# Down and output products with the weights standing and 512 tokens streamed, in a gated mix of linear attention and a GEGLU network

## The chip, the cores and the metric

The kernel runs on one core of one Trainium2 chip. Its engines are TensorE (PE in the profile, with its weight loads shown as PEld), VectorE (DVE), ScalarE (ACT), GpSimd (POOL) and SyncE (SP), which here only issues DMAs. The metric is device microseconds for one launch. Most executions of one kernel agree within 0.3%.

## The reference, cut to what matters

```python
x = A_x                                              # 2048 tokens x 640
g = sigmoid((x * gate_w).sum(-1, keepdims=True))     # one number per token
a = linear_attention(x, wqkv, w_phi) @ wo            # 32 heads of 20
b = (gelu(x @ w_gate) * (x @ w_up)) @ w_down         # hidden size 1728
return g * a + (1 - g) * b                           # 2048 x 640, bf16
```

The change touches the last two products, the one with `wo` and the one with `w_down`, which the kernel adds up in the same accumulator, the factor (1 - g), and the way the result goes to memory. The attention part is divided by its denominator and multiplied by g / (1 - g) before, so that one multiplication by (1 - g) closes both.

## The kernel before, in words

The 2048 tokens are 16 tiles of 128, and four tiles are one block. All is written out by hand: a small scheduler (`_Sched`) emits each instruction in program order on its engine's queue and puts a semaphore wait ahead of it for what it reads and overwrites. The order of the program is therefore the order of every queue, and a waiting instruction holds all that stand behind it on its engine. DMAs of the SP queue go round 16 lanes.

The program has three stages. `attention_state` projects keys, values and queries and builds the state of the linear attention. `ffn` first runs gate and up for 4 blocks x 14 chunks of the hidden size (counter `n`, 0 to 55): for each chunk ten 128x512 matmuls (L469), a GELU on ACT (L857) and a product on DVE (L861), which leaves the hidden activations transposed in `hT`, with the hidden index on the partitions and the block's 512 tokens along the row. Chunk 13 holds only 64 hidden rows; its product (L851) is written to partitions 0 to 63 and again to 64 to 127, half of the tokens each (`odd`) in blocks 0 to 2. Between the chunks stand the attention's last steps: `q_turn(t)` (a transposing DMA on SP), `num(t)` (eleven matmuls at L878 into PSUM banks 2 and 3, three DVE operations that leave `Og`, and a transposing DMA that leaves `goT`). After the fourth chunk of block 0 `kv_state` reads the attention state out of banks 3 and 4, and `gates` computes the gate column `Gm`.

The third stage is `down_pair`, called for two token tiles at a time, eight times. All its matmuls (L921) have 64 rows. The two halves of the array work side by side: rows 0 to 63 for one accumulator bank, rows 64 to 127 for the other, and such a couple is called a slot below. The standing operand is a 64x128 piece of `hT` (or `goT`); the streamed one is 320 columns of `wd_sb` (or `wo_sb`). A group is one pair of banks. Each group is opened (14 chunks of `hT` and 5 of `goT`: 19 slots) and later closed with the halves swapped (13 and 5: 18 slots). ACT scales the bank by `Gm[:, t]`, one number per partition (L936), into `outsb`, and one DMA per two tiles writes 320 KB out. The last pair has three groups of 320, 224 and 96 columns, and DVE takes half of their evacuations (L933).

Of the kernel before, what the change touches and what calls it, by code (L numbers as in the profile page):

```python
# [3 lines left out]
P = 128  # L4
BF16 = mybir.dt.bfloat16
F32 = mybir.dt.float32
AF = mybir.ActivationFunctionType
ALU = mybir.AluOpType
# [99 lines left out]
class _Kernel:  # L108
    S, D, H, DH, F = 2048, 640, 32, 20, 1728
    KD = D // P  # L110
    NT = S // P
    TB = 4
    BT = TB * P
    NB = S // BT
    NFC = 14
# [35 lines left out]
    def alloc(self):  # L151
        nc = self.nc
        S, D, KD, NT, BT, NFC, DH = self.S, self.D, self.KD, self.NT, self.BT, self.NFC, self.DH
        T = nc.alloc_sbuf_tensor
        self.xT = T("xT", [P, KD, S], BF16)
        self.wo_sb = T("wo_sb", [P, KD, D], BF16)
        self.wg_sb = T("wg_sb", [P, KD, 13 * P], BF16)
        self.wu_sb = T("wu_sb", [P, KD, 13 * P], BF16)
        self.wgu_sb = T("wgu_sb", [P, KD, P], BF16)
        self.wd_sb = T("wd_sb", [P, NFC, D], BF16)  # L160
        self.Eq = T("Eq", [P, NT, self.G * P], BF16)
        self.KV = T("KV", [P, self.G, 72], BF16)
        self.hmask = T("hmask", [P, 3, self.HG], BF16)
        self.mask = T("mask", [P, KD, 8], BF16)
        self.ident = T("ident", [P, P], BF16)
        self.gz = T("gz", [P, P], BF16)
        self.gcol = T("gcol", [P, NT], F32)
        self.gtmp = T("gtmp", [P, NT], F32)
        self.Gm = T("Gm", [P, NT], F32)
        self.Gr = T("Gr", [P, NT], F32)  # L170
        self.BD = T("BD", [P, KD, 4 * DH], BF16)
        self.wphi_sb = T("wphi_sb", [P, KD, DH], BF16)

        def place(lists):
            size = {"b": 0}
            plans = []
            for items in lists:
                c = 0
                for name, shape, dt in items:
                    n = mybir.dt.size(dt)  # L180
                    for s_ in shape[1:]:
                        n *= s_
                    c = (c + 31) // 32 * 32
                    plans.append((name, shape, dt, c))
                    c += n
                size["b"] = max(size["b"], c)
            arena = T("arena%d" % len(self._arenas), [P, size["b"]], mybir.dt.uint8)
            self._arenas.append(arena)
            base = nc.lookup_mloc(arena).addr
            for name, shape, dt, c in plans:  # L190
                setattr(self, name, nc.alloc_sbuf_tensor_at(name, shape, dt, offset=base + c))
        self._arenas = []
        place([
            [("w3", [P, KD, self.K0 + 2 * self.H * self.E], BF16)],
            [("hT0", [P, NFC, BT], BF16), ("gl", [P, 3, BT], BF16)],
        ])
        place([
            [("Ek", [P, self.NSE, self.G * P], BF16), ("vaug", [P, self.NSV, self.G, 64], BF16)],
            [("hT1", [P, NFC, BT], BF16), ("RH", [P, 2, 2, self.H], F32), ("Dq", [P, self.NSQ, 2, self.G * self.HG], F32),
             ("Sb", [P, 2 * self.G * self.HG, 5], F32), ("Sc", [P, 2 * self.G * self.HG, 2], F32),  # L200
             ("between", [P, 1472], F32), ("Sa", [P, 2 * self.G * self.HG, 10], F32)],
        ])
        place([
            [("Eq0", [P, self.G * P], BF16), ("Dk", [P, self.NSE, 2, 2 * self.G * self.HG], F32)],
            [("hT2", [P, NFC, BT], BF16)],
        ])
        place([
            [("wkT", [P, KD, D], BF16), ("wqT", [P, KD, D], BF16), ("room", [P, 504], F32),
             ("wref", [P, KD, self.H], F32), ("rest", [P, 600], F32), ("xtok", [P, self.TB, D], BF16)],
            [("ahead", [P, 2 * KD, D], BF16), ("kstage", [P, self.HM * DH], F32)],  # L210
            [("upl", [P, len(self.LATE), BT], F32), ("qstage", [P, self.HM * DH], F32)],
            [("under", [P, 4464], F32), ("upf", [P, len(self.UP), BT], F32)],
            [("goT", [P, self.NGO, KD, P], BF16), ("Og", [P, 2, D], BF16), ("outsb", [P, 4, D], BF16)],
        ])
        self.ps = nc.alloc_psum_tensor("ps", [P, 4096], F32)

    def bank(self, b, n=512):
        return self.ps[:, b * 512:b * 512 + n]
# [603 lines left out]
    def gateup(self, b, c, banks):  # L822
        sc = self.sc
        xs = lambda kt: self.xT[:, kt, b * self.BT:(b + 1) * self.BT]
        xr = [("xT", t) for t in range(4 * b, 4 * b + 4)]
        old = (self.oldw, self.oldk, self.oldq, [("xT", t) for t in range(12)])[b]
        hT, hk = self.hT(b, c), b
        slot = self.gn % 3
        self.gn += 1
        if c < 13:  # L830
            i = 0 if c < 7 else 1
            early = c in self.UP + self.LATE
            done = early and b == 0
            if done and c != self.LATE[0]:
                banks = banks[::-1]
            for w, wk, bk in ((self.wg_sb, "wg", banks[0]), (self.wu_sb, "wu", banks[1]))[:1 if done else 2]:
                for kt in range(self.KD):
                    key = self.upheld(c)[1] if early and wk == "wu" else (wk, i, kt)
                    self.mm(bk, 0, 512, w[:, kt, c * P:(c + 1) * P], xs(kt), kt == 0, kt == self.KD - 1, xr + [key])
            up, upk = (self.upheld(c)[0], ("upf", c)) if done else (self.bank(banks[1]), ("ps", banks[1]))  # L840
            self.gateup_evac(b, c, banks[0], slot, up, upk, old)
        else:
            bk = banks[1 if b else 0]
            for kt in range(self.KD):
                self.mm(bk, 0, 512, self.wgu_sb[:, kt, :], xs(kt), kt == 0, kt == self.KD - 1, xr + ["wgu0", "wgu1"])
            sc.op("act", lambda e: e.activation(self.gl[64:128, slot, :], self.ps[0:64, bk * 512:bk * 512 + 512],
                                                AF.Gelu_apprx_tanh),
                  reads=[("ps", bk)], writes=[("gl", slot)], guard=self.oldw)
            for r in (0, 1):
                odd = lambda v: v if b == 3 else v.rearrange("p (u r q) -> p u r q", r=2, q=P)[:, :, r, :]  # L850
                sc.op("dve", lambda e: e.tensor_tensor(  # L851
                    odd(hT[64 * r:64 * r + 64, :]), odd(self.ps[64:128, bk * 512:bk * 512 + 512]),
                    odd(self.gl[64:128, slot, :]), ALU.mult),
                    reads=[("ps", bk), ("gl", slot)], writes=[("hT", hk, c, r)], guard=old)

    def gelu(self, bank, slot):
# [14 lines left out]
    def num(self, t, b):  # L871
# [4 lines left out]
        for g in range(self.G):  # L876
# [18 lines left out]
        sc.dma("sp", lambda e: e.dma_start_transpose(dst, self.Og[:, sl, :]), reads=[("Og", sl)],  # L895
               writes=[("goT", t)], guard=old + list(dead))

    def down_pair(self, t0, banks, last):

        sc = self.sc  # L900
# [25 lines left out]
        def evac(h):  # L926
            for j in (0, 1):
                t, w0, w = parts[h][j]
                bk, dst, g = banks[h][j], self.outsb[:, t % 4, w0:w0 + w], self.Gm[:, t:t + 1]
                rd, wr = [("ps", bk), "Gm"], [("outsb", t % 4, h, j)]  # L930
                was = [("outsb", t % 4, k, (t - t0)) for k in (0, 1)] if last and h < 2 else ()
                if last and j == 1:
                    sc.op("dve", lambda e: e.tensor_scalar(dst, self.bank(bk, w), g, None, op0=ALU.mult), reads=rd, writes=wr,  # L933
                          guard=was)
                else:
                    sc.op("act", lambda e: e.activation(dst, self.bank(bk, w), AF.Copy, scale=g), reads=rd, writes=wr,  # L936
                          guard=was)
# [4 lines left out]
                sc.dma("sp", lambda e: e.dma_start(self.out[t * P:(t + 1) * P, c0:c1], self.outsb[:, t % 4, c0:c1]),  # L942
                       reads=[("outsb", t % 4, h, j) for j in (0, 1)], writes=[("out", t0, h)])
            elif h == nw - 1:
                if t0 < self.TB:
                    rows = self.out[0:self.BT, :].rearrange("(p j) n -> p j n", j=self.TB)[:, t0:t0 + 2, :]
                else:
                    rows = self.out[t0 * P:(t0 + 2) * P, :].rearrange("(j p) n -> p j n", p=P)
                sc.dma("sp", lambda e: e.dma_start(rows[:, :, :], self.outsb[:, os_:os_ + 2, :]),
                       reads=[("outsb", os_ + j, k, j) for j in (0, 1) for k in range(nw)], writes=[("out", t0, h)])  # L950

# [22 lines left out]
    def ffn(self):  # L974
# [6 lines left out]
        n = 0  # L981
        for b in range(self.NB):
            for idx, c in enumerate(order):
# [17 lines left out]
                    if t < 2:  # L1001
                        self.q_turn(t)
                n += 1
        p = [(2, 3), (4, 5)]
        for t in range(0, self.NT, 2):
            final = t + 2 == self.NT
            for _ in self.down_pair(t, p + [(0, 1)] if final else p, final):
                pass
# [44 lines left out]
```

## Time and profile before

| | |
|---|---|
| median of 3 runs | 281.81 us (281.76 to 282.28) |
| the profiled execution | 281.94 us, span 280.7 us |
| granted TensorE clock | 1.00 over the whole span |
| PE busy | 276.9 us, 99% |
| DVE, ACT, POOL busy | 146.8, 106.3, 109.7 us |
| DMA | 24.08 MB, 59848 packets |
| stage of `down_pair` | 198.0 to 279 us |

The page gives busy time by engine, the span in 40 slices, the chain that ended last, and groups of instructions by line. In a timeline a row is a run of like instructions: its start, the time from there to the end of the last, its name and the count. Matmuls are pipelined, so the step from one row's start to the next row's start, divided by the count, is what one matmul really takes of PE; the mean ns in the groups is its latency.

### The profile page before, as it was taken

The numbers are of one execution on the slowest core, as the hardware profiler recorded it, in microseconds if no ns is written. First come the engines' busy times: TensorE is split into PE (matmuls) and PEld (weight loads), VectorE is DVE, ScalarE is ACT, GpSimd is POOL, SyncE is SP. The second block draws the span as 40 slices with busy tenths as digits, with TensorE's granted clock in tenths as the row PEclk, the third lists the DMA queues.
The fourth block names the chain that finished last, engine by engine and source line by source line (L and its number), as shares of the span: only waits on it lengthen the run. The fifth ranks groups of instructions, "written<-read, shape, count | busy, mean of one in ns | idle before, by whom it ended". The sixth has DMA issues, their size and how long they took to land.

```text
span 280.7 us, 6549 instructions
## 1 busy us (share of the span) xinstructions
PE 276.9 (99%) x2729; PEld 168.0 (60%) x2746; DVE 146.8 (52%) x242; ACT 106.3 (38%) x205; POOL 109.7 (39%) x173
## 2 busy tenths in 40 slices
PE   8999999999999999999999999999999999999997
PEld 5566766666665445444444444445677777777785
DVE  1756999999999976655575556655200000000001
ACT  3347978878784322222232223222021121122011
POOL 7937911101068999986666666300000000000000
DMA  7999989300000436554343344731100110110111
GB/s 210 230 221 194 250 274 343 94 2 0 2 0 0 55 75 126 88 112 79 75 79 75 77 79 85 88 75 26 23 22 29 49 47 2 49 49 4 49 49 47
DMA packets 59848, 24.08 MB, mean 86 GB/s; under 512 B 50858, under 2 KB 59306, under 8 KB 59818
## 3 DMA queue, kind: packets, MB, share of 16 engines
q1 hardware_dynamic: 59152, 23.63, 37.3%
q8 instruction: 21, 0.34, 0.5%
q10 hardware_dynamic: 666, 0.03, 0.2%
q14 instruction: 9, 0.07, 0.1%
HBM read 9.04 MB, written 2.62 MB: 42 GB/s over the span
## 4 chain that ended last, share of the span: by engine, by line
PE 99%; issue 0%; ACT 0%
PE ps L469 58%; PE ps L921 29%; PE ps L659 4%; PE ps L482 2%; PE ps L878 2%; PE ps L695 2%; PE ps L735 1%; PE ps L409 1%; PE ps L345 0%; ACT outsb L936 0%; PE ps L742 0%; PE ps L374 0%
## 5 line engine op out<-in xcount | busy, mean ns | idle before, releaser
L469 PE MATMUL ps<-xT,wu_sb 128*128 128x512 bf16 x250 | 62.8, 379 | 0.4
L469 PE MATMUL ps<-xT,wg_sb 128*128 128x512 bf16 x253 | 62.6, 379 | 0.5
L857 ACT ACTIVATE gl<-ps 128x512 bf16<-128x512 f32 x52 | 31.0, 597 | 74.1 <-PE ps L469 70.5
L469 PE MATMUL ps<-w,xT 128*128 128x368 bf16 (+6 forms) x340 | 51.6, 303 | 0.0
L921 PE MATMUL ps<-wd_sb,hT 64*128 64x320 bf16 x648 | 47.0, 296 | 0.0
L469 PEld LDWEIGHTS ps<-xT,wu_sb 128*128 128x128 bf16 x260 | 25.4, 98 | 30.3
L933 DVE TENSOR_SCALAR outsb<-ps,Gm 128x320 bf16<-128x320 f32 (+2 forms) x3 | 1.3, 440 | 78.9 <-ACT outsb L936 78.1
L469 PEld LDWEIGHTS ps<-w,xT 128*128 128x128 bf16 x340 | 32.1, 98 | 14.6
L936 ACT ACTIVATE outsb<-ps,Gm 128x320 bf16<-128x320 f32 (+2 forms) x31 | 14.5, 515 | 66.9 <-PE ps L921 66.9
L469 PEld LDWEIGHTS ps<-xT,wg_sb 128*128 128x128 bf16 x260 | 24.0, 97 | 26.4 <-issue 0.2
L921 PEld LDWEIGHTS ps<-wd_sb,hT 64*128 64x128 bf16 x648 | 31.5, 94 | 12.8 <-DVE Og L890 0.4
L861 DVE TENSOR_TENSOR hT<-ps,gl 128x512 bf16<-128x512 f32 x34 | 23.4, 689 | 23.5 <-PE ps L469 23.5
L627 POOL TENSOR_TENSOR Eq<-Eq,Dq 128x660 bf16<-128x660 bf16 x16 | 21.6, 1350 | 20.0 <-DVE Dq L620 19.3
L686 DVE TENSOR_TENSOR Ek<-Ek,Dk 128x1320 bf16<-128x1320 bf16 x16 | 25.9, 1620 | 0.5
L677 DVE TENSOR_REDUCE Dk<-Ek 128x66 f32<-128x1320 bf16 x16 | 24.3, 1519 | 2.3 <-ACT gcol L541 2.3
L551 ACT ACTIVATE Ek<-ps 128x627 bf16<-128x627 f32 x32 | 20.5, 693 | 6.0 <-PE ps L659 4.5
L608 POOL TENSOR_TENSOR Sa<-Eq 128x660 f32<-128x660 bf16 x16 | 21.9, 1368 | 1.6 <-ACT Ek L551 1.6
L551 ACT ACTIVATE Eq<-ps 128x627 bf16<-128x627 f32 x32 | 20.6, 705 | 2.4 <-PE ps L469 2.4
L301 POOL MEMSET Eq<- 128x1408 bf16 x16 | 19.7, 1297 | 0.0
L921 PE MATMUL ps<-wo_sb,goT 64*128 64x320 bf16 x240 | 19.2, 296 | 0.0
L701 POOL MEMSET Ek<- 128x66 bf16 x11 | 4.3, 393 | 38.2 <-PE ps L695 35.7
L608 POOL TENSOR_TENSOR Sb<-Sa 128x330 f32<-128x330 f32 x16 | 16.7, 1045 | 1.3
(92 smaller groups left out, 255.7 us busy)
## 6 DMA issues: line engine op xcount, KB each, us to landing
out_dram<-outsb SPq DMA_DIRECT2D x7, 320.0 KB, 2.3
wd_sb<-in_B_w_down_dram SPq DMA_DIRECT2D x1, 2080.0 KB, 11.0
wg_sb<-in_B_w_gate_dram SPq DMA_DIRECT2D x5, 224.0 KB, 4.0
wg_sb<-in_B_w_gate_dram SPq DMA_DIRECT2D x5, 192.0 KB, 4.1
wu_sb<-in_B_w_up_dram SPq DMA_DIRECT2D x5, 192.0 KB, 4.3
w<-in_A_wqkv_dram SPq DMA_DIRECT2D x5, 160.0 KB, 4.3
wo_sb<-in_A_wo_dram SPq DMA_DIRECT2D x1, 800.0 KB, 11.5
xtok<-in_A_x_dram SPq DMA_DIRECT2D x2, 320.0 KB, 3.2
```

Source lines behind the costliest of these rows:

```text
L301: self.sc.op("pool", lambda e: e.memset(self.Eq[:, t, :], 1.0), writes=[("Er", t, 0), ("Er", t, 1)])
L469: self.sc.op("pe", lambda e: e.matmul(self.ps[:, bank * 512 + c0:bank * 512 + c0 + n], lhs, rhs, start=first, stop=fin), reads=reads, writ ...
L551: self.sc.op("act", lambda e: e.activation(dst, src, AF.Exp, scale=scale), reads=[("ps", b), ("ps", b + 1)], writes=[(name, sl, s)])
L608: sc.op("pool", lambda e: e.tensor_tensor(out, x, y, ALU.add), reads=reads, writes=writes, guard=old)
L627: self.sc.op("pool", lambda e: e.tensor_tensor(v, v, ratio.unsqueeze(3).to_broadcast([P, G, HG, self.DH]), ALU.mult), reads=[("Dq", sl, 1) ...
L659: self.sc.op("pe", lambda e: e.matmul(out, self.xT[:, kt, t * P:(t + 1) * P], self.w3[:, kt, c:c + 2 * n].rearrange("p (r w) -> p r w", w= ...
L677: self.sc.op("dve", lambda e: e.tensor_reduce(self.Dk[:, se, 0, :].rearrange("p (u h) -> p u h", h=self.HG), self.k_view(se), AX.X, ALU.ad ...
L686: sc.op("dve", lambda e: e.tensor_tensor(v, v, R.rearrange("p (u h) -> p u h", h=self.HG).unsqueeze(3).to_broadcast([P, 2 * self.G, self.H ...
L857: self.sc.op("act", lambda e: e.activation(self.gl[:, slot, :], self.bank(bank), AF.Gelu_apprx_tanh), reads=[("ps", bank)], writes=[("gl", ...
L861: self.sc.op("dve", lambda e: e.tensor_tensor(self.hT(b, c), up, self.gl[:, slot, :], ALU.mult), reads=[upk, ("gl", slot)], writes=[("hT", ...
L921: sc.op("pe", lambda e: e.matmul(self.bank(bk, w), lhs, rhs, start=opens and x == 0, stop=end and not opens, skip_group_check=True), reads ...
L936: sc.op("act", lambda e: e.activation(dst, self.bank(bk, w), AF.Copy, scale=g), reads=rd, writes=wr, guard=was)
```

## The change

For blocks 0 to 2 the two operands change places. A new `down_turned(b, banks)` makes a 64x128 piece of `wd_sb` or `wo_sb` the standing operand, and streams the block's tokens of `hT` or `goT`: 512 at a time for output columns 0 to 511 (two groups, each with two banks of 128 output columns), and twice 256 for the last 128 columns (a third group). Opening and closing have the same 19 and 18 slots, but there are three groups for four tiles instead of four.

The result is now transposed, output column on the partition and token along the row. So the factor (1 - g) has to lie along the row: `gate_rows`, called after chunk 46, writes 12 columns of `Gm` to a scratch tensor in memory and reads it back to all 128 partitions (`GmB`, 6 KB each). DVE multiplies bank by `GmB` into `outT`, five transposing DMAs per block turn `outT` into `outsb`, and one DMA of 640 KB writes the block. `outT` and `GmB` lie in the part of `Eq` that is dead by then.

Block 3 keeps `down_pair`. Its evacuations now wait until block 2's out DMA has read `outsb`. Bank pairs are (4,5), (2,3) in this order, where they were (2,3), (4,5). In chunk 13 of blocks 0 to 2 both halves are now written for all 512 tokens.

```diff
+    def gate_rows(self):
+        n = self.NT - self.TB
+        sc, T = self.sc, self.TB
+        sc.dma("sp", lambda e: e.dma_start(self.gdram.rearrange("(p t) -> p t", p=P), self.Gm[:, 0:n]), reads=["Gm"],
+               writes=["gdram"])
...
+        sc.dma("sp", lambda e: e.dma_start(self.GmB, self.gdram.partition_broadcast(P)), reads=["gdram"],
+               writes=["GmB"], guard=[("Eq", t) for t in (8, 9, 10)])
...
+    def down_turned(self, b, banks):
...
+        parts = [((0, 0, BT), (1, 0, BT)), ((2, 0, BT), (3, 0, BT)), ((4, 0, H), (4, H, H))]
...
+            if c <= NFC:
+                lhs, rhs = self.wd_sb[a:a + 64, c, o * P:(o + 1) * P], self.hT(b, c)[a:a + 64, c0:c0 + w]
...
+                lhs, rhs = self.wo_sb[a:a + 64, k, o * P:(o + 1) * P], self.goT[a:a + 64, t0:t0 + nt, k, :]
...
+        opening, closing = list(range(NFC + 1)) + wos, list(range(NFC)) + wos
+        for opens, steps in ((True, opening), (False, closing)):
+            for h in range(3):
+                for x, c in enumerate(steps):
+                    for r in (0, 1):
+                        mm(r, r if opens else 1 - r, h, c, opens, x, len(steps))
...
+                    g = self.GmB.rearrange("p (q t) -> p t q", q=P)[:, t0:t0 + nt, :]
+                    sc.op("dve", lambda e: e.tensor_tensor(
+                        tiles(self.outT[:, o, c0:c0 + w]), tiles(self.bank(banks[h][j], w)), g, ALU.mult), reads=[("ps", banks[h][j]), "GmB"], writes=[("outT", o, j if h == 2 else 0)],
+                        guard=[("Eq", t) for t in (5, 6)])
+                for o in ((0, 1), (2, 3), (4,))[h]:
+                    sc.dma("sp", lambda e: e.dma_start_transpose(self.outsb[:, :, o * P:(o + 1) * P], self.outT[:, o, :]),
...
+        sc.dma("sp", lambda e: e.dma_start(rows, self.outsb[:, :, :]),
...
-                was = [("outsb", t % 4, k, (t - t0)) for k in (0, 1)] if last and h < 2 else ()
+                was = [("outsb", t % 4, o) for o in range(self.KD)]
...
+                if n == 47:
+                    self.gate_rows()
-        p = [(2, 3), (4, 5)]
-        for t in range(0, self.NT, 2):
+        p = [(4, 5), (2, 3)]
+        for b in range(self.NB - 1):
+            self.down_turned(b, [(4, 5), (2, 3), (0, 1)] if b % 2 == 0 else [(4, 5), (2, 3), (6, 7)])
+        for t in range(self.NT - self.TB, self.NT, 2):
```

More of the change, by code (lines that the diff above doesn't have):

```diff
@@ L215, in alloc @@
         self.ps = nc.alloc_psum_tensor("ps", [P, 4096], F32)
+        self.gdram = nc.dram_tensor("gate_rows", [(NT - self.TB) * P], F32, kind="Internal").ap()
     def bank(self, b, n=512):
@@ L849, in gateup @@
             for r in (0, 1):
-                odd = lambda v: v if b == 3 else v.rearrange("p (u r q) -> p u r q", r=2, q=P)[:, :, r, :]
                 sc.op("dve", lambda e: e.tensor_tensor(
-                    odd(hT[64 * r:64 * r + 64, :]), odd(self.ps[64:128, bk * 512:bk * 512 + 512]),
-                    odd(self.gl[64:128, slot, :]), ALU.mult),
+                    hT[64 * r:64 * r + 64, :], self.ps[64:128, bk * 512:bk * 512 + 512],
+                    self.gl[64:128, slot, :], ALU.mult),
                     reads=[("ps", bk), ("gl", slot)], writes=[("hT", hk, c, r)], guard=old)
@@ L896, in num @@
                writes=[("goT", t)], guard=old + list(dead))
+    def gate_rows(self):
[3 more added lines that the diff above has]
+               writes=["gdram"])
+        self.GmB = self.Eq[:, 7:10, :].rearrange("p a b -> p (a b)")[:, 0:2 * n * P].bitcast(F32)
+        sc.dma("sp", lambda e: e.dma_start(self.GmB, self.gdram.partition_broadcast(P)), reads=["gdram"],
+               writes=["GmB"], guard=[("Eq", t) for t in (8, 9, 10)])
+        self.outT = self.Eq[:, 4:6, :].rearrange("p a b -> p (a b)")[:, 0:self.D * T].rearrange("p (o c) -> p o c", o=self.KD)
@@ new lines, in down_turned, with mm @@
+    def down_turned(self, b, banks):
+        sc, NFC, KD, BT = self.sc, self.NFC - 1, self.KD, self.BT
+        H = BT // 2
+        parts = [((0, 0, BT), (1, 0, BT)), ((2, 0, BT), (3, 0, BT)), ((4, 0, H), (4, H, H))]
+        wos = [NFC + 1 + k for k in range(KD)]
+        def mm(r, j, h, c, opens, x, n):
+            o, c0, w = parts[h][j]
+            bk, a, end = banks[h][j], 64 * r, x == n - 1
+            if c <= NFC:
+                lhs, rhs = self.wd_sb[a:a + 64, c, o * P:(o + 1) * P], self.hT(b, c)[a:a + 64, c0:c0 + w]
+                rd = [("hT", b, c), "wd"] if c < NFC else [("hT", b, 13, r), ("wd13", r)]
+            else:
+                k, t0, nt = c - NFC - 1, self.TB * b + c0 // P, w // P
+                lhs, rhs = self.wo_sb[a:a + 64, k, o * P:(o + 1) * P], self.goT[a:a + 64, t0:t0 + nt, k, :]
+                rd = [("goT", t) for t in range(t0, t0 + nt)] + ["wo"]
+            out = self.bank(bk, w)
+            sc.op("pe", lambda e: e.matmul(out if c <= NFC else out.rearrange("p (t q) -> p t q", q=P), lhs, rhs,
+                                           start=opens and x == 0, stop=end and not opens, skip_group_check=True),
+                  reads=rd, writes=[("ps", bk)] + ([("turn", bk)] if end else []), signal=end,
+                  after=[("turn", bk)] if x == 0 and not opens else ())
+        opening, closing = list(range(NFC + 1)) + wos, list(range(NFC)) + wos
[4 more added lines that the diff above has]
+                        mm(r, r if opens else 1 - r, h, c, opens, x, len(steps))
+                if opens:
+                    continue
+                for j in (0, 1):
+                    o, c0, w = parts[h][j]
+                    t0, nt = self.TB * b + c0 // P, w // P
+                    tiles = lambda v: v.rearrange("p (t q) -> p t q", q=P)
+                    g = self.GmB.rearrange("p (q t) -> p t q", q=P)[:, t0:t0 + nt, :]
[4 more added lines that the diff above has]
+                    sc.dma("sp", lambda e: e.dma_start_transpose(self.outsb[:, :, o * P:(o + 1) * P], self.outT[:, o, :]),
+                           reads=[("outT", o, j) for j in ((0, 1) if h == 2 else (0,))], writes=[("outsb", t, o) for t in range(4)],
+                           guard=self.before_num())
+        if b == 0:
+            rows = self.out[0:BT, :].rearrange("(p j) n -> p j n", j=self.TB)
+        else:
+            rows = self.out[b * BT:(b + 1) * BT, :].rearrange("(j p) n -> p j n", p=P)
+        sc.dma("sp", lambda e: e.dma_start(rows, self.outsb[:, :, :]),
+               reads=[("outsb", t, o) for t in range(4) for o in range(KD)], writes=[("out", b)])
@@ L944, in evac @@
             elif h == nw - 1:
[L945 to L948, printed above, removed]
+                rows = self.out[t0 * P:(t0 + 2) * P, :].rearrange("(j p) n -> p j n", p=P)
                 sc.dma("sp", lambda e: e.dma_start(rows[:, :, :], self.outsb[:, os_:os_ + 2, :]),
```

## The prediction

> **What bounds the kernel now.** I read the page's busy shares and chain first, then PE's timeline at three places, then DVE and SP around the places that the change touches. The page:
>
> ```profile
> span 280.7 us, 6549 instructions
> ...
> PE 276.9 (99%) x2729; PEld 168.0 (60%) x2746; DVE 146.8 (52%) x242; ACT 106.3 (38%) x205; POOL 109.7 (39%) x173
> ...
> PE ps L469 58%; PE ps L921 29%; PE ps L659 4%; PE ps L482 2%; PE ps L878 2%; PE ps L695 2%; PE ps L735 1%; PE ps L409 1%; PE ps L345 0%; ACT outsb L936 0%; PE ps L742 0%; PE ps L374 0%
> ```
>
> PE is the bound from end to end; the products to be changed are 29% of the chain. So only two things can move the time: what one slot takes of PE, and new waits of PE. PE's timeline, in the gate and up stage, in the products, and in the last pair:
>
> ```profile
> 99.24 1.24 PE L469 MATMUL ps<-xT,wg_sb 128*128 128x512 bf16 x5
> ...
> 104.63 0.38 PE L469 MATMUL ps<-xT,wu_sb 128*128 128x512 bf16 x1
> ```
>
> ```profile
> 196.80 1.24 PE L469 MATMUL ps<-xT,wu_sb 128*128 128x512 bf16 x5
> 197.97 3.98 PE L921 MATMUL ps<-wd_sb,hT 64*128 64x320 bf16 x56
> ```
>
> ```profile
> 276.00 1.41 PE L921 MATMUL ps<-wd_sb,xT 64*128 64x224 bf16 x26
> 277.24 0.64 PE L921 MATMUL ps<-wo_sb,Eq 64*128 64x224 bf16 x10
> 277.72 0.72 PE L921 MATMUL ps<-wd_sb,xT 64*128 64x96 bf16 x26
> 278.27 0.38 PE L921 MATMUL ps<-wo_sb,Eq 64*128 64x96 bf16 x10
> ```
>
> The reader is to divide steps between starts by slots. A 512-wide matmul on all rows: (104.63 - 99.24) / 25 = 0.2156 us. A slot of two 224-wide halves: (277.72 - 276.00) / 18 = 0.0956. Of two 96-wide ones: 0.55 / 13 = 0.0423. For 320 columns the out DMAs count best, two pairs of 74 slots apart:
>
> ```profile
> 209.29 0.35 SPq L949 DMA_DIRECT2D out_dram<-outsb  x1
> ...
> 229.40 40.58 SPq L949 DMA_DIRECT2D out_dram<-outsb  x5
> ```
>
> (229.40 - 209.29) / 148 = 0.1359. From 96 to 224 columns the slope is 53.3 / 128 = 0.416 ns a column, which leaves 0.0423 - 96 x 0.000416 = 0.0024 us fixed in each slot. Weight loads cost nothing: two per slot fit even into 0.0423.
>
> DVE in block 0, weight loads at the start of the products, and the DMAs that serve as prices:
>
> ```profile
> 88.46 0.88 DVE L851 TENSOR_TENSOR hT<-ps,gl 64x256 bf16<-64x256 f32 x2
> ...
> 91.63 0.15 DVE L716 TENSOR_TENSOR KV<-ps,hmask 128x2 bf16<-128x2 f32 x1
> ```
>
> ```profile
> 197.97 0.25 PEld L921 LDWEIGHTS ps<-wd_sb,hT 64*128 64x128 bf16 x6 [0.42 <-DVE Og L890]
> ```
>
> ```profile
> out_dram<-outsb SPq DMA_DIRECT2D x7, 320.0 KB, 2.3
> ...
> Eq<-Og SPq DMA_TRANSPOSE x4, 2.6
> ```
>
> **The change part by part. Slots.** Columns streamed are the same: before 4 groups x 37 slots x 320 per block, after 37 x (512 + 512 + 256). Only the number of slots falls, 148 to 111. Before: 148 x 0.1359 = 20.11 us per block. After: a 512-wide slot is not in the trace; I take 0.2156, the row of the same width, and for 256 columns 0.0956 + 32 x 0.000416 = 0.1089, so 37 x (2 x 0.2156 + 0.1089) = 19.98. The gain is 0.13 per block, 0.38 for three; counted as 37 slots saved x 0.0024 x 3 it is 0.27. I take 0.33. Bounds: none of the fixed part left, 512 x 0.416 = 0.2130 and 0.1065, gives 19.70 per block, a gain of 1.2; widths in proportion, 0.1359 x 1.6 = 0.2174 and 0.1087, gives 20.11, a gain of zero. The streamed `goT` has four runs of 128; the nearest row with runs, 2 x 240 columns (L659), has no gap of its own.
>
> **Start of the products.** The first slot begins at 197.97, where 196.80 + 5 x 0.2156 = 197.88 was possible: it waits for `Og` of tile 15 in banks 2 and 3, which the weight-load row names. Opened with (4,5), whose readers end with the product at 193.44 + 0.69, nothing is late; (2,3) come 19 x 0.216 = 4.1 us later. Gain 0.09, no more than this step.
>
> **Chunk 13, on DVE.** Two 64x256 operations (426 ns) become 64x512, as block 3 already has them (694 ns): 0.54 us more per block. Blocks 1 and 2 have DVE gaps of 1.47 us per chunk. In block 0 DVE runs without a gap from 84 to 99 us, and `kv_state` is behind: its last read of bank 4 ends at 91.63 + 0.15 = 91.78, and PE writes that bank at 92.45 (chunk 7: five matmuls before 93.52). The slack of 0.67 shrinks to 0.13. What a released wait takes to reach PE: `Og` ended at 197.69 and the load came at 197.97, 0.28. So the loss is 0 to 0.15; I take 0.10, nearer to the only row. Later banks have over a microsecond. POOL's `q_scale(0)` waits for the DVE step behind chunk 13 and slips 0.54; `q_turn(0)`, issued at 91.83 and landing 3.5 later, has until 98.9.
>
> **Gate rows, on SP.** Two DMAs between `goT(12)` (issued at 179.54) and `q_turn(15)` (182.49): the second waits for the first to land, by the 48 KB row 1.5 us, so `q_turn(15)` slips by about a microsecond and lands, 3.5 us after issue, near 187; beside the 786 KB broadcast perhaps at 190. `num(15)` needs it at 195.4. Nothing, with 5 us of cover; beyond that PE waits one for one. `goT(13)` behind it waits for its `Og` until 186.3 anyway.
>
> **Evacuation.** ACT loses 8 x 523 ns per block; DVE gets four 128x512 products (nearest row L861, 689 ns) and two of 256 (426): 3.6 us in 20, on an engine that is idle after 198.8. A bank is wanted again 5.8 us or more after its closing. Nothing.
>
> **Transposes and the way out.** Five transposes and one DMA a block: 5 x 1.2 us of SP issue in 20 us. What counts is the turn to block 3 at time S, because its evacuations wait for block 2's out DMA. The third group's closing starts 18 x 0.109 = 2.0 before S. With X the time of a 512-wide DVE product, the second group's evacuation begins at S - 1.7 (latency 0.3) and ends at S - 1.7 + 2X; the third's ends one X later, at the earliest S + 0.2 + X. For X = 0.69 that is S + 0.9; SP is held by two transposes until S + 1.4, the fifth lands 2.6 later at S + 4.0, the 640 KB land by S + 7.4 (2.3 for 320 KB, and 1.1 more for the second half). Block 3's first evacuation is due at S + 56 x 0.1359 + 0.3 = S + 7.9, and the last pair opens on its banks at S + 74 x 0.1359 = S + 10.1, less 1.05 for two ACT copies and a signal: S + 8.8. Cover 1.4 us; nothing.
>
> The Trainium skill, "SBUF — State Buffer", section "Door 1: The DMA port swizzle", says that SBUF has lines of 16 bytes and that each access to a new line costs extra; `GmB` is read in steps of 48 bytes. It gives no size; at double time, X = 1.38, the estimate from it stays within the cover, and the sum is the same. The nearest row is L886, which reads PSUM in steps of 84 bytes, 128x32 in 177 ns, against 195 for L620's contiguous 33: no penalty there.
>
> **Sum.** 281.94 - 0.33 - 0.09 + 0.10 = 281.62 for an execution like the profiled one, which was 0.13 above the median: 281.49, 0.11% less. About 0.2% (0.56 us) is what a measurement of this kernel can tell from no change, so this is on the small side of it.
>
> **Rivals.** *The fixed part goes away.* If two wide halves hide it, the slot gain is 1.2 and the time 281.81 - 1.2 - 0.09 + 0.10 = 280.6. For it: it is unknown what the 2.4 ns are. Against: full-row 512-wide matmuls still show them, 0.2156 against 0.2130.
>
> *The last pair waits for block 2's way out (slower).* The third evacuation may end up to S + 2.9 (5.95 for the fifth transpose and the out DMA before S + 8.8); 3X - 1.7 passes that from X = 1.5 us on, and each 0.1 of X beyond costs 0.3. At X = 2.2 PE idles 2.0 us at the opening of the last pair: 283.5. The same happens if transposes and out DMA together take 1.4 us longer than their rows. For it: a strided f32 operand is in no DVE row here, and `outsb` is a strided target. Against: L861 with an f32 operand in SBUF (upf) took 1.0 us in the mean, beside a busy POOL, and POOL is idle here.
>
> *Wide slots save nothing.* In proportion, as bounded above: 281.81 - 0.09 + 0.10 = 281.8, no change. Against: 0.0956 for 224 columns is already more than in proportion.
>
> **How the numbers follow.** The forecast, with its spread of 281.2 to 281.8, gets 0.62; of it 0.17 falls below 281.25 by the scatter of runs and 0.45 within 0.2%. The fixed part going away 0.14, faster. The wait at the last pair 0.14, slower. Nothing saved 0.08, of which 0.06 within 0.2% and 0.02 slower. A loss in block 0 of more than the bounds say 0.02, slower. So faster 0.31, same 0.51, slower 0.18. The range 281.0 to 282.3 leaves out most of the first and second rival.
>
> **What would show it.** The step per 512-wide slot in the new product rows: 0.216 confirms the forecast, 0.213 the first rival, 0.217 the third. The first row of the products 0.09 nearer to the last L469. A gap in PE of at most 0.15 near 92.4. The DVE evacuation at 0.7 us; the out DMA of block 2 landing before S + 8.8 and no idle PE at the opening of the last pair. The prediction is wrong if PE's slots or one of these waits is off by more than half a microsecond.

## The result and the profile after

The changed kernel takes 282.77 us in the median of 22 runs (281.81 to 283.29), the kernel before 281.77 (281.43 to 282.36). The ratio is 1.0030 with a 95% interval of 1.0022 to 1.0038: 1.0 us slower, where 0.3 us faster was forecast, and outside the range of 281.0 to 282.3. The profiled execution took 282.74 us, with a span of 281.5.

Two lines of the page of the changed kernel, the busy times and the chain that ended last, by line:

```profile
PE 278.0 (99%) x2524; PEld 156.9 (56%) x2524; DVE 163.6 (58%) x260; ACT 94.9 (34%) x181; POOL 109.9 (39%) x173
...
PE ps L470 58%; PE ps L927 21%; PE ps L982 4%; PE ps L660 4%; PE ps L483 2%; DMA out_dram<-outsb 2%; PE ps L878 2%; PE ps L696 2%; PE ps L736 1%; DMA outsb<-Eq 1%; SPq L949 1%; PE ps L410 1%; PE ps L346 0%; ACT outsb L997 0%; DVE Eq L945 0%
```

PE is still at 99%, but the chain no longer runs over PE alone: DMAs stand in it, a write to `out_dram` and a transpose into `outsb`. (L927 is the new product, L982 the old one in block 3, L945 the new evacuation, L997 ACT's.) PE's timeline of the changed kernel shows where:

```profile
196.75 1.24 PE L470 MATMUL ps<-xT,wu_sb 128*128 128x512 bf16 x5
197.93 3.19 PE L927 MATMUL ps<-hT,wd_sb 64*128 64x512 bf16 x28
...
202.04 3.19 PE L927 MATMUL ps<-hT,wd_sb 64*128 64x512 bf16 x28
...
206.14 1.69 PE L927 MATMUL ps<-hT,wd_sb 64*128 64x256 bf16 x28
...
208.22 2.97 PE L927 MATMUL ps<-hT,wd_sb 64*128 64x512 bf16 x26
...
257.97 3.97 PE L982 MATMUL ps<-wd_sb,xT 64*128 64x320 bf16 x56
...
267.34 0.84 PE L982 MATMUL ps<-wo_sb,Eq 64*128 64x320 bf16 x10
```

The slots do what was forecast: (206.14 - 202.04) / 19 = 0.2158 us with 512 columns and 2.08 / 19 = 0.1095 with 256. The three blocks take 257.97 - 197.93 = 60.04 us, against 60.32 before (197.97 to 258.29, the start of block 3): 0.28 gained. The kernel before at that place:

```profile
258.29 1.93 PE L921 MATMUL ps<-wd_sb,xT 64*128 64x320 bf16 x26
```

The chain in order of time shows what follows in the changed kernel at the turn to block 3:

```profile
259.96 2.46 DMA outsb<-Eq
...
262.51 4.99 DMA out_dram<-outsb
...
267.65 0.95 ACT outsb L997 x2
268.60 0.05 issue
268.65 10.33 PE ps L982 x213
```

Block 2's fifth transpose and its out DMA land one after the other, at 267.50; only then may ACT empty the first pair's banks into `outsb`, and the last pair starts at 268.65 instead of 267.34 + 5 x 0.136 = 268.02. That is 0.63 us of idle PE (a lone first half starts in between, at 268.23). The rest is behind the last matmul, which starts at 278.76; the span ends 2.74 us later, and in the kernel before it was 278.45 and 2.23.

| part of the span, us | before | after | difference |
|---|---|---|---|
| up to the first product | 197.97 | 197.93 | -0.04 |
| products of blocks 0 to 2 | 60.32 | 60.04 | -0.28 |
| block 3, to the last matmul's start | 20.16 | 20.79 | +0.63 |
| from there to the end | 2.23 | 2.74 | +0.51 |

The sum is +0.82, the difference of the spans; the medians differ by 1.0, because the execution profiled before was 0.17 us above its median. So the question was why the out DMA took 5.0 us and why the end became longer, where nothing of it was changed. The DMA view of the changed kernel from 262.5 to 268 us, its line of GB/s in 40 slices of 0.14 us and its line of the instruction queue:

```profile
GB/s 0 0 0 0 0 0 65 335 354 363 354 372 335 354 363 363 363 335 510 252 56 0 0 0 0 9 9 9 9 9 19 28 19 0 0 0 0 0 0 0
...
q8 instruction: 1, 0.02, 1.1%
```

All but a trickle has passed by 265.4. Of the 16 DMA engines that each raise the semaphore, 15 have done so at 265.71 and the last at 267.50. In the same window one packet of the instruction queue, 16 KB, went by: it started at 265.11 and took 0.94 us. The same view of the end, 276 to 282 us, has one such packet after (at 278.65) and none before. The trace has 20 such packets, and between two of them lie 205 to 308 of TensorE's recorded instructions, 258 in the mean. From this came theory F: each 16 KB fetch of TensorE's instructions goes through one of the 16 engines, takes about a microsecond and holds up that engine's share of a DMA under way. (Which engine carried a packet is not in the traces; that it is the late one is inferred.) The change removes 439 TensorE instructions (the program has 5527 before, 5088 after), and so moves all later fetches; one now falls on block 2's out DMA, another on the end. Rival D was that the way out is too long in itself, and the end is scatter.

### The profile page after: what moved, and what is told of

Read it like the earlier page. It is cut to its first block, busy times and chain, and to the rows that moved or that the text cites. A ratio compares the mean times of both kernels' runs of the same rounds, so it can differ in the third digit from the quotient of the medians.

```text
span 281.5 us, 6146 instructions
## 1 busy us (share of the span) xinstructions
PE 278.0 (99%) x2524; PEld 156.9 (56%) x2524; DVE 163.6 (58%) x260; ACT 94.9 (34%) x181; POOL 109.9 (39%) x173
## 4 chain that ended last, share of the span: by engine, by line
PE 94%; DMA 3%; SPq 1%; ACT 0%; DVE 0%; issue 0%; ACTq 0%
PE ps L470 58%; PE ps L927 21%; PE ps L982 4%; PE ps L660 4%; PE ps L483 2%; DMA out_dram<-outsb 2%; PE ps L878 2%; PE ps L696 2%; PE ps L736 1%; DMA outsb<-Eq 1%; SPq L949 1%; PE ps L410 1%; PE ps L346 0%; ACT outsb L997 0%; DVE Eq L945 0%
## 5 line engine op out<-in xcount | busy, mean ns | idle before, releaser
L470 PE MATMUL ps<-xT,wu_sb 128*128 128x512 bf16 x260 | 64.1, 379 | 0.0
L470 PE MATMUL ps<-xT,wg_sb 128*128 128x512 bf16 x260 | 63.9, 378 | 0.0
L927 PE MATMUL ps<-hT,wd_sb 64*128 64x512 bf16 (+1 forms) x486 | 46.8, 340 | 0.0
L945 DVE TENSOR_TENSOR Eq<-ps,Eq 128x512 bf16<-128x512 f32 (+1 forms) x18 | 15.3, 903 | 45.2 <-PE ps L927 45.2
L861 DVE TENSOR_TENSOR hT<-ps,gl 128x512 bf16<-128x512 f32 x34 | 23.3, 689 | 22.0 <-PE ps L470 21.8
L927 PEld LDWEIGHTS ps<-hT,wd_sb 64*128 64x128 bf16 x486 | 23.6, 94 | 20.6 <-ACT gl L857 0.4
L997 ACT ACTIVATE outsb<-ps,Gm 128x320 bf16<-128x320 f32 (+2 forms) x7 | 3.1, 490 | 78.7 <-DMA out_dram<-outsb 70.1
L927 PE MATMUL ps<-goT,wo_sb 64*128 64x512 bf16 (+1 forms) x180 | 19.2, 340 | 0.0
```

The lines of the kernel that those rows point to most:

```text
L470: self.sc.op("pe", lambda e: e.matmul(self.ps[:, bank * 512 + c0:bank * 512 + c0 + n], lhs, rhs, start=first, stop=fin), reads=reads, writ ...
L861: self.sc.op("dve", lambda e: e.tensor_tensor(self.hT(b, c), up, self.gl[:, slot, :], ALU.mult), reads=[upk, ("gl", slot)], writes=[("hT", ...
L927: sc.op("pe", lambda e: e.matmul(out if c <= NFC else out.rearrange("p (t q) -> p t q", q=P), lhs, rhs, start=opens and x == 0, stop=end a ...
L945: sc.op("dve", lambda e: e.tensor_tensor(tiles(self.outT[:, o, c0:c0 + w]), tiles(self.bank(banks[h][j], w)), g, ALU.mult), reads=[("ps", ...
```

## The experiments

### 192 satisfied waits: the fetches moved, nothing else

```diff
                 for kt in range(self.KD):
+                    if b > 0 and kt in (1, 2, 3) and self.pad > 0:
+                        self.pad -= 1
+                        for k in ("act", "dve"):
+                            sc.engs["pe"]["obj"].wait_ge(sc.engs[k]["sem"], 1)
                     key = self.upheld(c)[1] if early and wk == "wu" else (wk, i, kt)
...
-        self.gn = 0
+        self.gn, self.pad = 0, 192
```

> The changed kernel with 192 waits that are already satisfied put in front of gate and up matmuls of blocks 1 and 2, so that each later 16 KB fetch of TensorE's instructions comes 192 instructions earlier. Theory F (the fetch goes over one of the 16 DMA engines and holds up that engine's share of whatever DMA is under way): no fetch falls on block 2's out DMA or on the last out DMAs any more, the out DMA lands about 3.3 us after its issue instead of 5.0, PE idles less than 0.1 us at the opening of the last pair (0.64 in the changed kernel), from the last matmul's start to the end 2.2 us (2.74), ratio to before 0.9985 to 0.9995. Rival D (the way out is too long by itself, DVE product 1.05 us and 640 KB in 4.1 us, and the end is scatter): stall of 0.5 us or more stays, ratio 1.002 to 1.003. If the waits themselves cost time, PE's steps in blocks 1 and 2 grow over 0.216 us per matmul.

Each insertion is one instruction on TensorE's queue (the trace has 39 semaphore instructions of TensorE in the changed kernel, 231 here). Measured: 281.34 us (281.12 to 282.0), ratio 0.9990, interval 0.9981 to 0.9999. In the profile the fetches are at 257.4, 265.9 and 273.0 us. The DMA view of this run, again 262.5 to 268 us, and its waits of ACT:

```profile
GB/s 0 0 0 0 0 0 0 0 0 9 317 363 354 382 344 344 391 344 382 354 372 344 335 131 119 0 0 0 0 0 0 0 0 0 0 0 0 0 0 0
```

```profile
266.32 0.94 ACT L1001 ACTIVATE outsb<-ps,Gm 128x320 bf16<-128x320 f32 x2 [68.78 <-DMA out_dram<-outsb]
```

The out DMA, issued at 262.95, lands at 266.18 after 3.2 us, with no trickle; a fetch stands in this window too, but it begins when the data are through. ACT still ends its wait on that DMA, yet 1.3 us earlier, which is inside the cover: block 3 takes 20.16 us as before the change, and the last stretch 2.18. The blocks take 60.04. F holds and D falls: the DVE product takes 1.06 us as in the changed kernel, the out DMA is even issued 0.44 us later (262.95 against 262.51), and the stall is gone. That later issue is a fetch's too: the one at 257.42 meets the third transpose, whose issue takes SP 1.65 us instead of 1.19. The version is faster than the changed kernel, 0.9990 against 1.0030. Over the kernel before it gains 0.10%, with an interval that just leaves out zero; the run with both edits below, whose fetches stand in about the same places, does not repeat that gain.

### A buffer of its own for block 3: the wait taken away

```diff
-                bk, dst, g = banks[h][j], self.outsb[:, t % 4, w0:w0 + w], self.Gm[:, t:t + 1]
+                bk, dst, g = banks[h][j], self.own[:, t % 4, w0:w0 + w], self.Gm[:, t:t + 1]
...
-                was = [("outsb", t % 4, o) for o in range(self.KD)]
+                was = [("hT", 0, c) for c in range(13)]
...
         p = [(4, 5), (2, 3)]
+        self.own = self.hT0[:, 0:5, :].rearrange("p c t -> p (c t)").rearrange("p (t d) -> p t d", d=self.D)
```

> The changed kernel, block 3's evacuations into a buffer of their own (the dead hT of block 0), so that nothing of block 3 waits for block 2's out DMA. Fetches stay where they are. Both theories: no idle PE at the opening of the last pair, 0.64 us less than the changed kernel. F: the end stays 0.5 us long, because the last fetch still falls on the last out DMAs: ratio to before about 1.001 (1.000 to 1.002). D: 0.999 to 1.000.

Measured: 281.72 us, ratio 1.0002 (0.9993 to 1.0011). Block 3 takes 20.16 us; the out DMA of block 2 is still late (issued at 262.20, last engine at 267.04, a fetch at 264.31), and nobody waits for it. The ratio alone would fit both theories. The end stays long, 2.65 us, with a fetch at 277.67. So the stall is the wait for `outsb`, and the late landing is not caused by block 3.

> Both edits together. F: neither the wait nor the late end: ratio to before 0.9985 to 0.9993, the same as with the 192 waits alone. D: the same as with the buffer alone.

Both edits together: 281.65 us, ratio 0.9997 (0.9988 to 1.0006), block 3 20.16 us and end 2.18 in the profile. The trace is as expected; the median is above the expected 0.9993 and its interval covers both that and the run with the waits alone. Once the fetch is moved, the buffer gains nothing that this measurement shows. So with the fetches out of the way the ratio is 0.9990 in one run and 0.9997 in the other.

### The kernel before with a fetch put on its end

> The kernel before with 73 satisfied waits, which makes its number of TensorE instructions equal to that of the changed kernel modulo 256 (5527 + 73 = 5088 + 512), so that a last fetch falls on its end as well. F: one more 16 KB fetch at about 278.5 us, one of the last out DMAs lands 0.5 to 1 us late, 0.3 to 0.6 us longer: ratio 1.001 to 1.002. D: no change, 0.9995 to 1.0005.

The same insertion in the kernel before, with 73. Measured: 282.31 us, ratio 1.0021 (1.0011 to 1.0031). The last part of its trace, the DMA view from 276 to 282 us:

```profile
q8 instruction: 1, 0.02, 1.1%
...
out_dram<-outsb SPq DMA_DIRECT2D x1, 160.0 KB, 3.1
```

The fetch begins at 277.66, and the 160 KB of the last pair's first group need 3.1 us, against 1.8 in the kernel before; the last stretch is 2.67 us instead of 2.23. By the medians a kernel whose work was not touched became 0.6 us slower through 73 waits. (The profiled execution itself took 281.64 us, because its products began at 197.25 instead of 197.97; the 0.44 us at the end is read from the last stretch alone.)

> Control: the kernel before with the same 192 satisfied waits. They cost nothing where TensorE's queue runs ahead, and no fetch falls on its end either way: ratio 0.9995 to 1.0005. If the waits themselves gained something, 0.998.

The control: 281.89 us, ratio 1.0006 (0.9997 to 1.0015), end 2.23, blocks 0 to 2 60.32. The interval takes in no change; the waits gain nothing by themselves, so they do not explain the first experiment. Here a fetch at 260.77 makes one 320 KB out DMA land 2.3 us late, at 263.91, and nothing waits for it.

The ten traces together leave little to chance. From the last matmul's start to the end, the five with a fetch within 0.8 us of that start take 2.54 to 3.05 us, the five without one 2.18 to 2.23. Of the 179 DMAs that landed after 200 us, 27 have a last engine more than 0.2 us behind the fifteenth, and in each of these a fetch was under way between issue and landing. But a late engine is not the only way in which a fetch costs time. The changed kernel's very last DMA, 48 KB, has none: its 16 engines land from 281.29 to 281.46. It is late because SP's issue of it, begun at 279.37 with the fetch under way, took 0.92 us, where it took 0.33 in the kernel before. All 16 issues of SP after 200 us that took over 1.23 us (transposes) or over 0.39 (other DMAs) had a fetch under way. Why the issue waits, the traces do not say.

### Twelve TensorE instructions fewer

```diff
-        for n in (512, 512, 512, 512, 512, 512, 128, 128, 128):
+        for n in (512, 512, 512, 512, 512, 512, 384):
...
-        for i in range(3):
+        for i in range(1):
...
-                sc.op("pe", lambda e: e.matmul(self.bank(b, P), ones[a:a + 64, 0:P], ones[a:a + 64, 0:P], start=True,
+                sc.op("pe", lambda e: e.matmul(self.bank(b, 3 * P), ones[a:a + 64, 0:P], ones[a:a + 64, 0:3 * P], start=True,
```

> The changed kernel with 12 TensorE instructions fewer: warm-up matmuls at the start merged into as many columns (three of 128 into one of 384, twice three of 128 into one of 384). Nothing else moves. Theory F: the fetch that fell five instructions before the end does not come any more, so the end after the last matmul falls from 2.74 to 2.2 us; the fetch in block 3 comes 12 x 34 ns = 0.4 us later, at 265.5, when block 2's out DMA is nearly through, so the stall at the last pair falls from 0.64 to 0 to 0.4. Ratio to before 0.999 to 1.0005. Without F: as the changed kernel, 1.002 to 1.004.

Half a miss. Measured: 282.11 us, ratio 1.0011 (1.0001 to 1.0020). The fetch in block 3 moved to 265.62, the out DMA landed at 266.19, and the stall is gone (block 3 20.16 us). But the last fetch did not stay away: it came at 278.77, 0.7 us after the last matmul's start, and the end became 3.05 us. The ratio lies between the two ranges expected. So the number of instructions executed does not say exactly where the last fetch falls: in this trace no instruction of TensorE is recorded behind it. How far ahead of its use a block is fetched was not measured.

### What the evacuation's stride costs

```diff
-        sc.dma("sp", lambda e: e.dma_start(self.gdram.rearrange("(p t) -> p t", p=P), self.Gm[:, 0:n]), reads=["Gm"],
+        sc.dma("sp", lambda e: e.dma_start(self.gdram.rearrange("(t p) -> p t", p=P), self.Gm[:, 0:n], allow_slow_non_contiguous=True), reads=["Gm"],
...
-                    g = self.GmB.rearrange("p (q t) -> p t q", q=P)[:, t0:t0 + nt, :]
+                    g = self.GmB.rearrange("p (t q) -> p t q", q=P)[:, t0:t0 + nt, :]
```

> The changed kernel with the gate rows laid out so that DVE reads them contiguously (memory scratch written tile by tile, 1536 single elements) instead of in steps of 48 bytes. If the step costs: the 128x512 product falls from 1.05 to 0.7 us. If the f32 operand in SBUF costs, 1.05 stays. The fifth transpose of block 2 is issued 0.4 us earlier at 0.7.

DVE's groups in the products stage, first the changed kernel (steps of 48 bytes), then this one (contiguous):

```profile
L945 DVE TENSOR_TENSOR Eq<-ps,Eq 128x512 bf16<-128x512 f32 x12 | 12.2, 1055 | 45.2 <-PE ps L927 45.2
```

```profile
L945 DVE TENSOR_TENSOR Eq<-ps,Eq 128x512 bf16<-128x512 f32 x12 | 7.7, 686 | 48.6 <-PE ps L927 48.6
```

The step costs 0.37 us for 512 elements; read contiguously, the f32 operand costs nothing (686 ns, and 691 for L861 with its bf16 one). The expected 0.4 us earlier issue of the fifth transpose did come: 266.01 with block 3 at 264.39, 1.62 us behind it instead of 1.99. The run as a whole is much slower, 288.32 us, for a reason that belongs to the edit: written as 1536 single elements, the scratch write is issued at 181.16 and SP waits until 192.73 for it to land, `q_turn(15)` is issued at 193.17 instead of 183.73, and PE waits for it. PE's timeline of this run:

```profile
199.03 0.75 PE L878 MATMUL ps<-KV,Eq 128*128 128x63 bf16 x11 [3.10 <-DMA Eq<-Eq]
199.61 2.30 PE L470 MATMUL ps<-xT,wg_sb 128*128 128x512 bf16 x5
...
203.98 0.98 PE L927 MATMUL ps<-hT,wd_sb 64*128 64x512 bf16 x4
```

### The bank order alone

```diff
-        p = [(2, 3), (4, 5)]
+        p = [(4, 5), (2, 3)]
```

> The kernel before with the banks of the first pair of groups as (4,5), (2,3) and nothing else. If the wait for Og of tile 15 set the start of the products, as the prediction said, the step from the last gate and up row's start to the first product falls from 1.17 to 1.08 us. If it is what the array takes to go from full rows to two halves, it stays 1.17, as in the changed kernel (196.75 to 197.93).

PE's timeline of the kernel before with this one edit:

```profile
196.51 1.24 PE L469 MATMUL ps<-xT,wu_sb 128*128 128x512 bf16 x5
197.69 2.48 PE L921 MATMUL ps<-wd_sb,hT 64*128 64x320 bf16 x34
```

The step is 1.18 us, as with the old order and in the changed kernel. Banks that are free do not shorten it, so it was not the wait for `Og`. That it is the change from full rows to two halves of the array fits, but is not shown: no run took that change away. Its one execution took 281.63 us.

## Why the prediction was wrong, point by point

**Slots: right.** 0.33 us was taken and 0.28 measured, with 0.2158 us per wide slot where 0.2156 was taken from the full-row matmul. By the prediction's slope of 0.416 ns a column 2.8 ns of this are fixed. The fixed part of a slot stays (first rival: no), and fewer slots do save it (third rival: no).

**Start of the products: the step failed, 0.09 us.** The row named `Og` as the releaser of the weight load, and the sum took the idle time as that wait. The run with the bank order alone shows no gain: the step stays at 1.18 us.

**Chunk 13: right place, smaller.** PE's step to chunk 7's first matmul is 243 ns in the changed kernel where 216 are usual: 0.03 us, inside the bounds of 0 to 0.15, where 0.10 was taken.

**Gate rows: right.** `q_turn(15)` was issued at 183.73, 1.2 us later than before, and PE did not wait. That PE would wait one for one beyond the cover was wrong: the contiguous variant idled 3.1 us and then lost at least 2.2 us more, because its next ten matmuls took (203.98 - 199.61) / 10 = 0.437 us each, twice the usual.

**Evacuation: the term was mis-sized, 1.06 us for 0.69.** The step weighed a rule against a row and took the row, and the cost that the rule calls for was there. The Trainium skill, "SBUF — State Buffer", section "Door 1: The DMA port swizzle", says that an access to a new 16-byte line costs extra; the runs show 0.37 us for 512 elements at 48 bytes. No other step was run, so that the line of 16 bytes is the reason is not shown. The row taken against it, L886, reads PSUM, and only 32 elements. The error used up 0.37 us of the cover, but did not decide: with the step in place and the fetch elsewhere there is no stall.

**Transposes and the way out: the step that failed.** The prediction put the danger in the right place, block 3's evacuations waiting for block 2's out DMA, and gave a cover of 1.4 us; it was the slower rival with 0.14. With block 3 at S = 257.97 the fifth transpose landed at S + 4.5 (4.0 predicted, 0.4 of it from the stride), the out DMA's 15 engines at S + 7.7 (7.4 predicted) and the sixteenth at S + 9.5. The run with 192 waits has it whole at S + 8.2, inside S + 8.8, and 0.44 of that is the fetch on its third transpose. So the rows priced the path to within 0.4 us. The step that failed is the term "Cover 1.4 us; nothing": it counted the landing by the rows' medians, with no engine late, and 0.63 us of idle PE stood in its place. What broke the cover was a transfer that no line of the kernel issues. Whether it falls on this DMA depends on the count of TensorE's instructions, which the prediction did not follow: the run with 192 waits has no stall. The limit itself does not follow from 10.1 - 1.05 as written, which is 9.05, but it holds: 1.15 us passed from the landing to the last pair, which puts it at S + 8.9. The rival's own condition, a DVE product of 1.5 us, was not met; its side condition, a way out 1.4 us longer than its rows, was.

**What was not in the sum at all: the end.** The last out DMAs have no term in the sum, since they are not changed; that put them at nothing. The fetch that fell on them cost 0.51 us in the profile; put on the kernel before, 0.44 in the profile and 0.6 in the median.

**Together:** 0.28 gained and 0.04 from the start of the run, against 0.63 and 0.51 lost. With the fetches out of the way the ratio is 0.9990 and 0.9997 in two runs, whose intervals both take in the 0.9989 of the prediction's sum. The sum of the change was near, in part by luck: the 0.09 that did not come at the start was nearly made good by the 0.07 that chunk 13 did not cost. What was left out is the instruction stream around it.

## What to carry to other kernels

An edit that changes the number of instructions moves every later instruction fetch, and a fetch that meets a short DMA which is waited for, the last output above all, can cost more than the edit gains, as it did here (1.14 us against 0.28): look for the instruction queue's packets in the windows where a DMA is on the path, before and after. A cover for a DMA should be counted with one late engine, up to 2.3 us here, not with the median landing. And a releaser in a row names what came last, not what would have been saved: changing that one thing alone is a cheap test.

## What the runs showed of the hardware

- In both kernels the 16 KB packets on the instruction queue are spaced 205 to 308 of TensorE's recorded instructions (means 255 before and 258 after; some records are missing), and adding 73 or 192 TensorE instructions moved them. One packet took 0.88 to 1.56 us. The Trainium skill, "Runtime: NRT & Kernel Launch", section "Instruction fetch mechanics", says that an engine's instructions are refilled in blocks of 16 KiB, 256 instructions, by a DMA queue, and calls the cost mostly hidden. The traces agree on the block. On the cost, no wait of TensorE is put down to a fetch in these traces, but DMAs beside it landed late, by 1.8 us (267.50 against 265.71), 2.3 us (263.91 against 261.63) and 0.7 us at the end (281.11 against 280.38). SP's issue of a DMA took longer under a fetch as well (0.92 us against 0.33).
- A DMA's landing is that of its slowest engine: in the three cases named, 15 of 16 engines landed within 0.2 us of each other.
- In the contiguous variant PE waited 3.1 us; the granted clock fell from 1.00 to 0.50 at 197.94 us, inside that wait, and was back at 1.00 at 204.77. The ten gate and up matmuls between took twice the usual time.
- A pair of 64-row matmuls keeps 2.4 to 3.0 ns per slot from 96 to 512 columns over a slope of 0.416 ns a column (0.0423, 0.1095 and 0.2158 us at 96, 256 and 512).
